# ELU steps whose relu VectorE takes from PSUM, and another order of all operations, in an attention kernel with a feed-forward layer behind it

## The chip, the cores and the metric

The kernel runs on one core of a Trainium2 chip. A core has five engines that each work through a queue of their own, in order: TensorE (PE in the profile, with PEld for its weight loads), VectorE (DVE), ScalarE (ACT), GpSimd (POOL) and SyncE (SP). They wait for each other by semaphores. Matrix products land in PSUM; ScalarE and VectorE carry them to SBUF. In this kernel POOL issues nearly all loads, SP issues the transposing loads and the stores. The metric is the time of one execution on the device, in microseconds.

## The reference

Eight batches of eight heads; 576 queries, 576 keys and 16 "beacon" keys that every query sees; the other keys are causal. The result of attention, 4608 tokens of 512 values, goes through a layer with an ELU between two products.

```python
def _attn_ref(q, k, v, beacon_k, beacon_v):
    B, H, S, D = q.shape                      # 8, 8, 576, 64
    k_all = np.concatenate([beacon_k, k], axis=2)
    v_all = np.concatenate([beacon_v, v], axis=2)
    scores = (1.0 / np.sqrt(D)) * np.matmul(q, k_all.transpose(0, 1, 3, 2))
    scores = np.where(causal, -1000000000.0, scores)
    a = np.exp(scores - scores.max(-1, keepdims=True))
    a /= a.sum(-1, keepdims=True) + 1e-09
    return np.matmul(a, v_all)

def _moe_ref(x, w_in, w_out):                 # 4608 x 512, 512 x 2048, 2048 x 512
    h = x @ w_in
    g = np.where(h > 0.0, h, np.exp(np.minimum(h, 0.0)) - 1.0)
    return g @ w_out
```

## The kernel before

The kernel is a set of small step functions and one long string of words, each word a step with its arguments. The program is issued in the order of that string, so every engine's queue is written out by hand: an engine does its share of the steps in the order in which they stand, and waits where a step's data or its buffer is not there yet. Neither a planner nor a loop decides at run time.

Attention, batch b: `lq` loads q and k (batches 0 to 2; `T` transposes them on TensorE, `cq` on VectorE or `ck` on ScalarE copies them out of PSUM), or `lk` copies them to a scratch in DRAM from which `lt` loads them transposed by DMA (batches 3 to 7); `cb` and `lp` put the beacon keys beside them. `lv` loads v in five pieces. `S` multiplies keys by queries, in the order of keys first, into a PSUM tile of two banks; `x` takes its exp on ScalarE; `m` masks on VectorE. The sums over the keys are matmuls with ones: `L` makes them for one group of four heads. For batches from BD = 3 on, `D` first adds the exps of the key blocks on VectorE, four additions for each pair of heads, so that `L` needs one matmul for each head in place of five. `n` makes the reciprocals (ln, then exp, on ScalarE), `W` multiplies v by the exps, and `M` scales the result into the tile `xT`. For batch 0 the work is cut into two halves, A and B.

The layer, tile t of 512 tokens (tiles 0 and 1 have 256): `F` makes one of 16 blocks of h in a PSUM bank of the tag hps, which has two. Then comes the ELU step of the block, in one of two forms. The usual one is `e` (exp, ScalarE, line 522), `u` (relu, ScalarE, line 527) and `k` (VectorE, line 537), min(exp - 1, relu). The one that spares ScalarE is `e`, then `r` on VectorE (min(exp, 1) - 1, line 545 for tiles 0 to 5 and line 549 for tiles 6 and 7), then `g` on VectorE (max of h from PSUM and r, line 554). The second product is `G` for tiles 0 and 1 (line 563) and `o`, `s` for the output. For tiles 2 to 9 it is a form of Strassen with seven products for eight: `Z` (VectorE) makes sums of blocks of g, `Q` (line 627) the matmuls, `J` takes partial results from PSUM, on ScalarE, or on VectorE where its word ends in `.v`. `wt` and `H` make the sums of weights. Tiles 8 and 9 use the same seven products for the first layer too: `X`, `P` (line 697), `K`, and the ELU of the blocks as `E`, `U` (ScalarE, line 726, or VectorE where the word ends in `.v`, line 728) and `V`.

`warm` and `wm` are dummy matmuls on zeros that keep TensorE busy in the head, four to a word. F.0.2 is the first step of the layer; all of the steps before it are called the head here. W.1.0 is batch 1's first product with v, L.2.0 batch 2's first step of sums that also reads v.

The buffers that matter: two PSUM tiles each for the tags S, hps and ops; three SBUF tiles for the exps and three for r and u. v has two buffers; so a third batch's load waits until the first batch's products are done.

Of the kernel before, what the change touches and what calls it, by code (L numbers as in the profile page):

```python
# [8 lines left out]
FP32 = mybir.dt.float32  # L9
# [8 lines left out]
def kernel(  # L18
# [11 lines left out]
    nc = tc.nc  # L30
# [144 lines left out]
    one32 = konst.tile([P, 1], FP32)  # L175
    nc.vector.memset(one32, 1.0)
# [225 lines left out]
    def L(b, g):  # L402
# [12 lines left out]
        else:  # L415
            t = hd[b, g] = psum.tile([P, 1024], FP32, tag="S", name="lt")
            r_ = lt[b, g] = t[:, 512 - QA:512 - QA + S]
            if b >= BD:
                for i in range(4):
                    nc.tensor.matmul(  # L420
                        out=r_[32 * i:32 * (i + 1), QA:S], lhsT=ones,
                        rhs=presum[b, 2 * g + i // 2][:, i % 2, QA:S], start=True, stop=True, skip_group_check=True)
            else:
                quad(b, g, QA, S, r_[:, QA:S], None, True)
# [91 lines left out]
    def flat(y):  # L516
        return y.rearrange("c n w -> c (n w)")
# [6 lines left out]
    @step  # L524
    def u(t, i):
        rb[t, i] = melt.tile([P, 512], FP16, tag="r", name="r")
        nc.scalar.activation(out=rb[t, i], in_=flat(hp[t, i]), func=AFT.Relu, bias=0.0, scale=1.0)  # L527
# [13 lines left out]
    @step  # L541
    def r(t, i):
        rb[t, i] = melt.tile([P, 512], FP16, tag="r", name="r")
        if t < 6:
            nc.vector.scalar_tensor_tensor(
                out=rb[t, i], in0=eb[t, i], scalar=1.0, in1=one32.to_broadcast([P, 512]),
                op0=ALU.min, op1=ALU.subtract)
# [243 lines left out]
    warm.4 warm.4 lq.0.0.0.4 lq.0.1.0.4 lv.0.2 warm.4 wm.4 ident T.0.0.0 bt ck.0.0.0 wm.4  # L791
    T.0.1.0 bk cb.0.2 cb.0.0 wm.4 lq.0.0.4.8 S.0.0.0 x.0.0.0 lq.0.1.4.8 T.0.0.1 lq.1.0.0.4 tri
    cq.0.1.0 cb.0.1 S.0.1.0 x.0.1.0 lv.0.0.1 T.0.1.1 wm.4 cq.0.0.1 S.0.0.2 x.0.0.2 S.0.0.1 wm.4
    cq.0.1.1 T.0.3.0 cb.0.3 x.0.0.1 cq.0.3.0 m.0.0.2 S.0.1.3 x.0.1.3 T.0.2.0 cq.0.2.0 S.0.1.1
    wm.4 x.0.1.1 T.0.2.1 S.0.3.0 wm.4 wm.4 x.0.3.0 T.0.3.1 cq.0.2.1 cq.0.3.1 S.0.2.0 wi.0
    S.0.2.3 x.0.2.0 wm.4 wm.4 x.0.2.3 wm.4 wm.4 m.0.0.0 m.0.2.0 m.0.1.0 S.0.3.1 x.0.3.1 wm.4
# [144 lines left out]
```

## Time and profile before

| | us |
|---|---|
| median of three runs | 334.65 (333.76, 334.65, 336.88) |
| the profiled execution, its own time | 336.74 |
| its span, first to last instruction | 335.0 |
| TensorE's mean granted clock | 0.993 of full speed |
| ScalarE, exps of the scores (line 336), 114 instructions | 105.7 |
| VectorE, k (line 537), 100 instructions | 67.0 |
| ScalarE, relu (line 527), 100 instructions | 61.9 |
| VectorE, g (line 554), 20 instructions | 13.7 |
| VectorE, r of tiles 0 to 5 (line 545), 14 instructions | 9.6 |

A row of a group gives the line, the engine, the operation, what it writes and reads, its shapes and its count, then the busy time, the mean of one in ns, and the time that the engine stood idle before such instructions with what ended it. A row of a stretch gives the busy time of each engine in it. The timeline gives start, length and what ran, in us from the start of the span. The profile is of one execution; the median is of others.

### The profile page before, as it was taken

The page shows a single profiled execution, that of the slowest core. Times are in us where ns is not written, and L with a number is a line of the kernel's source. Part 1 is how long each engine was busy: PE and PEld are TensorE (multiplying, and loading weights), DVE is VectorE, ACT ScalarE, POOL GpSimd, SP SyncE. Part 2 cuts the span into 40 slices and gives each one's busy share as a digit, 9 for nine tenths or more (in the row PEclk, how much of TensorE's full clock was granted, in tenths as well). Part 3 has the DMA queues.
Part 4 walks back from the last instruction along what each step waited for, and adds up shares of the span by engine and source line. Part 5 has one row for each costly group of instructions (what it writes and reads, how often), then busy time and mean ns, then how long its engine had stood idle before and what let it go on. Part 6 is the DMA issues. An engine that isn't in the chain of part 4 may idle for free.

```text
span 335.0 us, 8848 instructions
## 1 busy us (share of the span) xinstructions
PE 325.6 (97%) x3616; PEld 210.7 (63%) x3616; DVE 284.7 (85%) x601; ACT 278.1 (83%) x452; POOL 90.9 (27%) x117
## 2 busy tenths in 40 slices
PE   8899999999999999999999999999999999999994
PEld 3566766544455565656566656655666888788783
DVE  3555788875979999999899989998999999999982
ACT  2689999799999988999997998988987586889610
POOL 8968268630017284440061050000000000000000
PEclk9989999999999999999999999999999999999999
DMA  9999999999909999999199094320110110111112
GB/s 115 157 179 175 205 189 163 158 154 162 163 3 102 172 140 173 166 178 118 53 136 151 5 68 102 71 35 31 38 61 31 45 54 31 48 47 33 64 65 95
DMA packets 129113, 34.66 MB, mean 103 GB/s; under 512 B 112944, under 2 KB 127536, under 8 KB 129072
## 3 DMA queue, kind: packets, MB, share of 16 engines
q0 software_dynamic: 94944, 18.49, 68.8%
q1 hardware_dynamic: 33408, 15.34, 22.8%
q8 instruction: 28, 0.46, 0.6%
q10 hardware_dynamic: 720, 0.26, 0.3%
q14 instruction: 13, 0.11, 0.1%
HBM read 37.22 MB, written 15.34 MB: 157 GB/s over the span
## 4 chain that ended last, share of the span: by engine, by line
PE 87%; DVE 3%; ACT 3%; POOL 2%; DMA 2%; issue 1%; ACTq 0%; DVEq 0%; POOLq 0%
PE hps L512 30%; PE ops L627 29%; PE sc L321 8%; PE ut L378 6%; PE hps L697 5%; PE ops L563 4%; PE lt L378 2%; DMA kst<-in_k_dram 2%; ACT et L336 2%; POOL qst L136 1%; PE lt L420 1%; PE w L214 1%; PE tp L267 1%; PE ub L378 1%; DVE gt L554 1%
## 5 line engine op out<-in xcount | busy, mean ns | idle before, releaser
L512 PE MATMUL hps<-xT,w_in 128*128 128x512 f16 (+1 forms) x544 | 118.5, 354 | 0.3
L336 ACT ACTIVATE et<-sc 128x1024 f16<-128x1024 f32 (+2 forms) x114 | 105.7, 978 | 10.1 <-PE sc L321 9.5
L627 PEld LDWEIGHTS <-gt 128*128 128x128 f16 x768 | 73.3, 98 | 20.2 <-issue 3.7
L522 ACT ACTIVATE e<-hps 128x512 f32<-128x512 f32 x120 | 73.5, 620 | 13.8 <-PE hps L512 11.2
L512 PEld LDWEIGHTS <-w_in 128*128 128x128 f16 x544 | 50.6, 98 | 41.4 <-issue 4.4
L537 DVE SCALAR_TENSOR_TENSOR gt<-e,r 128x512 f16<-128x512 f32 x100 | 67.0, 684 | 8.0 <-ACT r L527 7.9
L527 ACT ACTIVATE r<-hps 128x512 f16<-128x512 f32 x100 | 61.9, 626 | 0.0
L627 PE MATMUL ops<-w_out,gt 128*128 128x256 f16 x384 | 50.7, 273 | 0.4 <-DVE gt L537 0.4
L627 PE MATMUL ops<-wt,gt 128*128 128x256 f16 x384 | 50.7, 273 | 0.0
L149 POOL DMA_DIRECT2D v<-in_v_dram x40 | 34.7, 919 | 5.0 <-DMA w_out<-in_moe_w_out_dram 2.7
L341 DVE TENSOR_TENSOR et<-et,triu 128x512 f16<-128x512 f16 (+4 forms) x108 | 31.2, 332 | 2.6 <-ACT et L336 2.4
L584 DVE TENSOR_TENSOR gt<-gt 128x1024 f16<-128x1024 f16 x48 | 32.4, 685 | 0.5
L378 PEld LDWEIGHTS <-v 128*32 128x32 f16 (+1 forms) x800 | 17.1, 96 | 10.6 <-issue 3.1
L394 DVE TENSOR_TENSOR qk<-qk,et 128x672 f16<-128x672 f16 (+2 forms) x60 | 21.2, 368 | 0.4
L378 PE MATMUL ut<-et,v 128*32 128x464 f16 (+3 forms) x560 | 20.9, 296 | 0.0
L472 DVE TENSOR_TENSOR xT<-ut,rl 128x672 f16<-128x672 f32 (+12 forms) x26 | 16.4, 670 | 3.1 <-PE ut L378 2.1
L643 DVE TENSOR_TENSOR osb<-ops,sm 128x512 f32<-128x512 f32 x24 | 16.4, 683 | 2.0 <-PE ops L627 1.9
L627 PE MATMUL ops<-w_out,s 128*128 128x256 f16 x128 | 17.1, 273 | 0.0
L563 PE MATMUL ops<-w_out,gt 128*128 128x512 f16 x64 | 16.0, 380 | 0.0
L736 DVE SCALAR_TENSOR_TENSOR gt<-e,r 128x512 f16<-128x512 f32 x24 | 15.9, 684 | 0.1
L627 PEld LDWEIGHTS <-s 128*128 128x128 f16 x128 | 12.3, 98 | 3.1 <-issue 0.3
L554 DVE TENSOR_TENSOR gt<-hps,r 128x512 f16<-128x512 f32 x20 | 13.7, 687 | 0.7
(111 smaller groups left out, 408.1 us busy)
## 6 DMA issues: line engine op xcount, KB each, us to landing
out_dram<-osb SPq DMA_DIRECT2D x35, 256.0 KB, 2.3
v<-in_v_dram POOLq DMA_DIRECT2D x24, 128.0 KB, 8.1
scr<-in_q_dram POOLq DMA_DIRECT2D x5, 576.0 KB, 15.6
scr<-in_k_dram POOLq DMA_DIRECT2D x5, 576.0 KB, 14.1
w_in<-in_moe_w_in_dram POOLq DMA_DIRECT2D x16, 128.0 KB, 5.9
w_out<-in_moe_w_out_dram POOLq DMA_DIRECT2D x4, 512.0 KB, 10.1
qst<-in_q_dram POOLq DMA_DIRECT2D x4, 288.0 KB, 8.7
kst<-in_k_dram POOLq DMA_DIRECT2D x4, 288.0 KB, 9.4
```

The costliest lines, as they stand in the source:

```text
L149: nc.gpsimd.dma_start(out=vt[b][r0:r0 + n, j, :, :], in_=v[b, :, ilo[j]:ilo[j] + n, :].rearrange("h s d -> s h d"),)
L321: nc.tensor.matmul(out=s[:, h, a - c0:e - c0], lhsT=t[D * h:D * (h + 1), 1, P * j:P * (j + 1)], rhs=t[D * h:D * (h + 1), 0, NB + qa + a - ...
L336: nc.scalar.activation(out=ets[b, d][:, :, a - EC2 * d:e - EC2 * d], in_=sc[b, g][:, :, a - c0:e - c0], func=AFT.Exp, bias=0.0, scale=SCALE)
L341: nc.vector.tensor_tensor(out=o, in0=o, in1=i, op=ALU.mult)
L378: nc.tensor.matmul(out=t[32 * i:32 * (i + 1), a - qa:e - qa], lhsT=ones[0:kc[j], :] if half is None else v16[0:kc[j], j, h, 32 * half:32 * ...
L512: nc.tensor.matmul(out=h[:, n_, :], lhsT=w_in16[:, cc, P * fc:P * (fc + 1)], rhs=xt[k][:, cc, a - TT * k:e - TT * k], start=(cc == 0), sto ...
L522: nc.scalar.activation(out=eb[t, i], in_=flat(hp[t, i]), func=AFT.Exp, bias=0.0, scale=1.0)
L527: nc.scalar.activation(out=rb[t, i], in_=flat(hp[t, i]), func=AFT.Relu, bias=0.0, scale=1.0)
L537: nc.vector.scalar_tensor_tensor(out=half(t, i), in0=eb[t, i], scalar=1.0, in1=rb[t, i], op0=ALU.subtract, op1=ALU.min)
L563: nc.tensor.matmul(out=ob[t, tb_], lhsT=gt[:, fc, P * tb_:P * (tb_ + 1)], rhs=w_out16[:, fc, :], start=(fc == 0), stop=(fc == NFC - 1))
L584: (nc.vector if eng == "v" else nc.gpsimd).tensor_tensor(out=o_, in0=a_, in1=b_, op=op_)
L627: nc.tensor.matmul(out=xy[t, n_][:, qd, :], lhsT=lw[:, P * qd:P * (qd + 1)], rhs=wt_[:, c, :], start=(first and qd == 0 and c == 0), stop= ...
```

## The change

Three things change. The ELU step that spares ScalarE in tiles 0 to 5 is no longer `e`, `r`, `g`: `u` gets an argument, and with `v` VectorE takes the relu from PSUM, always behind the exp of the same step; then comes `k`. In tiles 6 and 7 `r` and `g` stay, and the constant `one32` goes with the form that read it. Second, `L` takes the summed form for every pair of heads that has a `D`, not for batches from 3 on. Third, the string is another one.

```diff
-    one32 = konst.tile([P, 1], FP32)
-    nc.vector.memset(one32, 1.0)
@@ L
-            if b >= BD:
+            if (b, 2 * g) in presum:
@@ u
-    def u(t, i):
+    def u(t, i, eng="s"):
         rb[t, i] = melt.tile([P, 512], FP16, tag="r", name="r")
-        nc.scalar.activation(out=rb[t, i], in_=flat(hp[t, i]), func=AFT.Relu, bias=0.0, scale=1.0)
+        if eng == "s":
+            nc.scalar.activation(out=rb[t, i], in_=flat(hp[t, i]), func=AFT.Relu, bias=0.0, scale=1.0)
+        else:
+            nc.vector.tensor_scalar(out=rb[t, i], in0=flat(hp[t, i]), scalar1=0.0, scalar2=None, op0=ALU.max)
@@ r
-        if t < 6:
-            nc.vector.scalar_tensor_tensor(
-                out=rb[t, i], in0=eb[t, i], scalar=1.0, in1=one32.to_broadcast([P, 512]),
-                op0=ALU.min, op1=ALU.subtract)
-        else:
-            nc.vector.tensor_scalar(
-                out=rb[t, i], in0=eb[t, i], scalar1=1.0, scalar2=1.0, op0=ALU.min, op1=ALU.subtract)
+        nc.vector.tensor_scalar(
+            out=rb[t, i], in0=eb[t, i], scalar1=1.0, scalar2=1.0, op0=ALU.min, op1=ALU.subtract)
```

Counted by words, the string differs so:

| steps | before | after |
|---|---|---|
| `u` on ScalarE, tiles 0 to 7 | 92 | 80 |
| `u` on VectorE (`.v`) | 0 | 24, in tiles 0 (5), 1 (5), 2 (6), 3 (1), 4 (4), 5 (3) |
| `r` and `g`, tiles 0 to 5 | 14 | 0 |
| `r` and `g`, tiles 6 and 7 | 6 | 8 |
| `k` | 100 | 112 |
| `D` (batch 2's first group of heads has 8 of them after) | 80 | 88 |
| `wm` | 18 | 12 |
| first copy of the head | `ck.0.0.0` | `cq.0.0.0` |

Of `J`, eight words lose their `.v` and three get one; of `U`, six lose it and four get it. The other words are the same, in another order. The order of POOL's loads, up to the first of batch 4:

```
before: lq.0.0.0.4 lq.0.1.0.4 lv.0.2 ident lq.0.0.4.8 lq.0.1.4.8 lq.1.0.0.4 tri lv.0.0.1 wi.0 lv.0.3.4 wi.1
        lq.1.0.4.8 wo.0 lq.2.0.4.8 lq.2.0.0.4 wo.1 lv.1.0.1 wo.2 lv.1.2.3.4 lv.2.2.3.4 wo.3 lp.4.0 lk.3.0
        lv.2.0.1 lk.3.1 lp.3.0 lp.3.1 lk.4.1 lk.4.0
after:  lq.0.0.0.4 lq.0.1.0.4 ident lq.0.0.4.8 lq.0.1.4.8 tri lq.1.0.0.4 lv.0.2 lv.0.0.1 wi.0 lv.0.3.4 wi.1
        lq.1.0.4.8 wo.0 wo.2 lq.2.0.4.8 lq.2.0.0.4 wo.1 lv.1.0.1 lk.3.1 lv.1.2.3.4 wo.3 lk.3.0 lk.6.0
        lp.3.1 lp.4.0 lv.3.2.3.4 lv.2.2.3.4 lv.2.0.1 lv.3.0.1 lk.4.0
```

The steps around F.0.2 in the two strings:

```
before: L.0.A S.0.0.3 S.0.2.1 x.0.0.3 x.0.2.1 wm.4 S.0.3.2 x.0.3.2 T.1.0.0 n.0.A T.1.1.0 wm.4 wm.4 W.0.A.0
        cb.1.0 cq.1.0.0 m.0.2.3 S.1.1 m.0.1.3 m.0.1.2 m.0.3.2 cb.1.1 ck.1.1.0 x.1.1 wm.4 wm.4 S.1.2 W.0.A.1 x.1.2 S.0.3.3 x.0.3.3 S.0.2.2 m.0.0.3 x.0.2.2
        M.0.A.0 M.0.A.1 F.0.2 e.0.2 u.0.2 k.0.2 lv.0.3.4
after:  S.0.0.3 x.0.0.3 L.0.A T.1.0.0 n.0.A cq.1.0.0 cb.1.3 T.1.1.0 ck.1.1.0 wm.4 m.0.0.3 S.1.2 lv.0.2 lv.0.0.1
        W.0.A.1 M.0.A.1 x.1.2 S.1.1 x.1.1 W.0.A.0 M.0.A.0 S.0.3.3 x.0.3.3 S.0.2.2 wi.0 F.0.2 x.0.2.2 S.1.5
        S.1.0 m.0.1.2 e.0.2 m.0.2.2 u.0.2 k.0.2
```

More of the change, by code (lines that the diff above doesn't have):

```diff
@@ L790 @@
     run("""
[L791 to L796, printed above, removed]
@@ L911 @@
-    Q.9.84.91 J.9.4 Q.9.91.98 Q.9.98.105 J.9.5 Q.9.105.112 Jh.9.1 Jh.9.0
+    warm.4 lq.0.0.0.4 warm.4 lq.0.1.0.4 warm.4 wm.4 ident wm.4 T.0.0.0 bt wm.4 bk wm.4 wm.4
+    T.0.1.0 cb.0.0 cq.0.0.0 S.0.0.0 x.0.0.0 T.0.1.1 lq.0.0.4.8 cq.0.1.0 cb.0.1 S.0.1.0 x.0.1.0
+    cq.0.1.1 wm.4 wm.4 T.0.0.1 S.0.1.1 S.0.1.3 x.0.1.1 T.0.3.0 x.0.1.3 lq.0.1.4.8 cq.0.0.1
+    S.0.0.2 x.0.0.2 T.0.2.0 cq.0.3.0 S.0.0.1 x.0.0.1 cb.0.2 cq.0.2.0 cb.0.3 T.0.2.1 S.0.3.0
+    T.0.3.1 cq.0.2.1 S.0.2.0 x.0.3.0 S.0.2.3 tri x.0.2.0 x.0.2.3 m.0.1.3 cq.0.3.1 m.0.2.0
@@ new lines @@
+    F.5.3 k.5.12 e.5.3 u.5.3 S.6.10 S.6.0 x.6.0 x.6.10 Q.4.98.105 F.5.9 e.5.9 u.5.9 k.5.3
+    Q.4.105.112 k.5.0 m.6.0.0 Z.5.3.0 S.6.6 J.4.6.v D.6.0.0 x.6.6 Z.5.3.1 k.5.9 m.6.0.1 S.6.8
+    x.6.8 Q.5.0.7 F.6.11 e.6.11 r.6.11 F.6.4 e.6.4 u.6.4 Q.5.7.14 g.6.11 S.6.12 lt.7.1 x.6.12
+    m.6.1.1 S.7.2 x.7.2 Z.5.1.0 F.6.5 lp.7.0 F.6.6 D.6.1.1 D.6.1.2 Z.5.1.1 e.6.5 e.6.6 u.6.5
+    Q.5.14.21 Q.5.21.28 S.6.11 S.7.4 x.7.4 Z.5.2.0 r.6.6 g.6.6 k.6.4 Z.5.2.1 F.6.15 F.6.14
+    e.6.15 D.6.0.1 D.6.0.2 J.5.0 e.6.14 m.6.2.1 D.6.0.3 u.6.15 Z.5.4.0 x.6.11 S.6.7 x.6.7
```

225 lines of the change are left out of this document (111 added, 114 removed).

## Prediction

> **What bounds the kernel now.** I read the page's busy shares and chain first, then the sums by stretches of 15 us.
>
> ```profile
> PE 325.6 (97%) x3616; PEld 210.7 (63%) x3616; DVE 284.7 (85%) x601; ACT 278.1 (83%) x452; POOL 90.9 (27%) x117
> PEclk9989999999999999999999999999999999999999
> DMA  9999999999909999999199094320110110111112
> PE 87%; DVE 3%; ACT 3%; POOL 2%; DMA 2%; issue 1%; ACTq 0%; DVEq 0%; POOLq 0%
> 15.00:30.00 15.00, 13.90 (x274) 10.11 (x269) 8.03 (x28) 12.89 (x18) 10.90 (x20) 0.89 1.32 173
> 30.00:45.00 15.00, 14.73 (x265) 10.79 (x263) 10.86 (x20) 14.97 (x25) 7.94 (x11) 1.00 1.27 202
> 45.00:60.00 15.00, 14.85 (x232) 9.72 (x234) 12.76 (x29) 14.25 (x21) 11.53 (x17) 1.00 1.94 169
> 60.00:75.00 15.00, 14.96 (x184) 7.07 (x174) 11.85 (x27) 12.78 (x21) 7.17 (x5) 1.00 2.21 156
> 285.00:300.00 15.00, 15.00 (x125) 11.91 (x123) 14.69 (x26) 13.13 (x27) 0.00 (x0) 1.00 0.16 54
> 315.00:330.00 15.00, 14.62 (x124) 11.78 (x123) 11.48 (x19) 4.21 (x8) 0.00 (x0) 1.00 0.16 54
> 27.88 1.05 PE L512 MATMUL hps<-xT,w_in 128*128 128x256 f16 x8
> ```
>
> TensorE is busy for 97% of the 335.0 us and is 87% of the chain that ended last. The columns of the stretches are length, PE, PEld, DVE, ACT, POOL, clock, DMA share, GB/s. Between 30 and 75 us TensorE lacks 0.46 us (0.27 + 0.15 + 0.04), in the stretch at the end 0.38; the stretches between are full, as 285 to 300 shows. So behind F.0.2, the first matmul of the ELU part at 27.88, sparing another engine cannot buy more than about 1 us: matmuls would have to go. What can move is the head before 27.88, where ScalarE or a load ends most waits and dummy matmuls fill TensorE. From 30 to 45 us ScalarE has 0.03 us free, so a faster head holds only if ScalarE follows. The DMA engines stand at nine tenths for most of the first 160 us: a load moved ahead pushes the ones behind it.
>
> **The relus and the engines' sums.**
>
> ```profile
> L545 DVE SCALAR_TENSOR_TENSOR r<-e,one 128x512 f16<-128x512 f32 x14 | 9.6, 688 | 2.6 <-ACT e L522 2.4
> L554 DVE TENSOR_TENSOR gt<-hps,r 128x512 f16<-128x512 f32 x20 | 13.7, 687 | 0.7
> L537 DVE SCALAR_TENSOR_TENSOR gt<-e,r 128x512 f16<-128x512 f32 x100 | 67.0, 684 | 8.0 <-ACT r L527 7.9
> L527 ACT ACTIVATE r<-hps 128x512 f16<-128x512 f32 x100 | 61.9, 626 | 0.0
> L728 DVE TENSOR_SCALAR r<-hps x1: 692/692/692, 314.1 to 314.1; 128x512 f16<-128x512 f32 x1
> L636 ACT COPY sm<-ops x15: 576/587/740, 106.8 to 320.0; 128x512 f32<-128x512 f32 x15
> L636 DVE COPY sm<-ops x9: 676/683/692, 115.1 to 325.4; 128x512 f32<-128x512 f32 x9
> L394 DVE TENSOR_TENSOR qk<-et 128x928 f16<-128x928 f16 x20 | 12.5, 634 | 0.4 <-PE lt L420 0.3
> L394 DVE TENSOR_TENSOR qk<-qk,et 128x672 f16<-128x672 f16 (+2 forms) x60 | 21.2, 368 | 0.4
> ```
>
> Rows of groups: count | busy, mean ns | idle before. Of the 20 steps that spare ScalarE (r, then g), 14 lie in tiles 0 to 5, 6 in tiles 6 and 7; after, 24 u on VectorE lie in tiles 0 to 5 and 8 r/g behind them. No 24 such relus are in the trace; the one relu that VectorE takes from PSUM costs 0.69 (L728). VectorE loses 14 x 0.69 (r) and 12 x 0.69 (g), 17.9 us; it gains 24 x 0.69 (relus), 12 x 0.68 (k) and 2 x 0.69 at most (r of tiles 6 and 7), 26.1, and the sums D of batch 2: two pairs, each 0.63 + 21.2/60 x 3 = 1.69, 3.4 us. Five of the copies J leave it (-3.4), two net U (up to -1.4), one copy of the head comes (0.7). Sum +7.5: 284.7 becomes 292. ScalarE loses 12 x 0.62 of relus (-7.4), but takes five J at 0.60, two U at 0.62: -3.2, and one copy of the head (the price of a J, 0.6) less: 278.1 becomes about 274. So "sparing ScalarE" is mostly given back; that it does so little is seen in the order itself.
>
> Where does it lie? In tiles 0 to 2 VectorE gains 16 x 0.69 + 10 x 0.68 - 10 x 1.37 + 3.4 = 7.6 us, against 9.5 us (4.1 + 2.2 + 3.2) that it had free from 30 to 75: covered, and tight; without cover it would be paid on TensorE. ScalarE loses four relus of tiles 0 and 1, 2.5 us, just where it was full. Each relu waits for the exp of its step, and VectorE's queue (k, masks) stands behind it; r stood behind the same exp, 2.6 us idle in 14 (L545), so the wait is no new one. The PSUM bank is free when the relu ends, before g would have ended: nothing lost. From 75 us on TensorE has no idle time to win; J and U there cost 0.
>
> **The head** (gain). Rows of the timeline: start, length, engine, what, idle time before and its releaser.
>
> ```profile
> 15.49 0.86 ACT L336 ACTIVATE et<-sc 128x832 f16<-128x832 f32 x1 [1.84 <-PE sc L321]
> 16.91 1.62 ACT L336 ACTIVATE et<-sc 128x832 f16<-128x832 f32 x2 [0.55 <-PE sc L321]
> 19.55 3.89 ACT L336 ACTIVATE et<-sc 128x832 f16<-128x832 f32 x5 [1.02 <-PE sc L321]
> 4.20 0.57 POOL L144 DMA_DIRECT2D v<-in_beacon_v_dram x1
> 4.72 0.94 POOL L149 DMA_DIRECT2D v<-in_v_dram x1
> 14.82 0.33 PE L267 MATMUL tq<-identb,kst 80*64 80x80 bf16 x8 [0.93 <-DMA kst<-in_k_dram]
> L161 POOL DMA_DIRECT2D w_in<-in_moe_w_in_dram x8: 532/536/565, 13.4 to 19.8; - x8
> DMA to landing us min/median/max: 4.9/6.4/7.4
> ```
>
> ScalarE stands idle 3.4 us (1.84 + 0.55 + 1.02) between the exps of batch 0, first for the last k load of batch 0. lv.0.2 (0.57 + 0.94 us on POOL) now stands behind all loads of batch 0, and tri ahead of lq.1: those loads start 1.5 us earlier, so 14.82 becomes about 13.3. The later two gaps stood behind dummy matmuls and score steps that the new order places behind exps ready earlier. I leave 0.7 us of idle, and 0.3 for the first exp, whose copy (cq.0.0.0) now queues on VectorE behind bk and cb: 3.4 - 0.7 - 0.3 = 2.4 gained (all kept 3.1; only the load's share 1.2). F.0.2 comes at 25.5; w_in has landed by then (19.8 + 4.9 = 24.7). The 24 dummy matmuls dropped lie in waits: 0.
>
> **Batch 2's sums** (gain). L.2.0 drops 16 of its matmuls.
>
> ```profile
> 82.74 0.90 PE L378 MATMUL lt<-et,ones 128*32 128x464 f16 x24
> 83.46 0.27 PE L378 MATMUL lt<-et,v 128*32 128x112 f16 x8
> L420 PE MATMUL lt<-qk,ones 128*32 128x464 f16 x40 | 3.8, 365 | 0.0
> ```
>
> Its 24 matmuls take 0.72 (82.74 to 83.46); four on a sum take 0.38 (3.8 over ten groups), of which some overlaps: -0.4 us (0 to -0.5).
>
> **The loads** (loss). POOL's queue now has lk.3.1 ahead of lv.1.2.3.4, and lk.3.0, lk.6.0 and lv.3.2.3.4 ahead of batch 2's v.
>
> ```profile
> 61.56 2.83 PE L378 MATMUL ut<-et,v 128*32 128x464 f16 x80
> L149 POOL DMA_DIRECT2D v<-in_v_dram x3: 730/873/891, 42.5 to 45.1; - x3
> DMA to landing us min/median/max: 8.9/9.7/10.0
> L760 POOL DMA_DIRECT2D scr<-in_q_dram x1: 2201/2201/2201, 53.2 to 53.2; - x1
> DMA to landing us min/median/max: 9.3/9.3/9.3
> L760 POOL DMA_DIRECT2D scr<-in_k_dram x2: 2511/2614/2718, 56.6 to 59.6; - x2
> DMA to landing us min/median/max: 12.5/13.3/14.1
> L760 POOL DMA_DIRECT2D scr<-in_q_dram x1: 2190/2190/2190, 62.9 to 62.9; - x1
> DMA to landing us min/median/max: 14.1/17.4/20.7
> ```
>
> Before, v of batch 1 landed at 45.1 + 8.9 = 54.0, and W.1.0 read it at 61.56: 7.6 us of slack. One lk costs the queue 4.6 (69.1 = 56.6 + 12.5 to 73.7 = 59.6 + 14.1), so v lands at 58.6, less up to 0.8 for the earlier start of the queue: I take 58.2. W.1.0 comes earlier by 2.4 and by F.1.6 and L.1.1, now behind it (about 1.0 each): 57.2. A wait of 1.0 us (0 to 1.6), with all of TensorE queued behind. Batch 2's v: three v pieces take 1.5 for two steps (52.5 to 54.0), 0.75 each. lk.3.0 landed 8.5 behind v of batch 1 (62.5) with three v pieces between; now 6.2 behind, 64.4. Then lk.6.0 (4.6) and seven pieces (5.3): 9.9. L.2.0 needs the last at 83.46 - 2.4 - 1.1 (F.2.2 and S.2.9 now stand behind it) + 1.0 = 81.0. At full speed it lands at 74.3. The copies landing at 73.7 and, beside the transposes, at 83.6 (62.9 + 20.7), took 14.5 for two, 1.58 times as long: 80.0. No wait, 1.0 us to spare.
>
> The Trainium skill, "DMA: Bandwidth & Descriptors", Queues, rings and completion order, says that each DMA engine takes turns between the queues that have work, packet by packet; the copy that landed at 83.6 fits a halved share, the one at 73.7 does not. By the rule alone the outcome would be the slower rival below.
>
> **Sum.** -2.4 - 0.4 + 1.0 = -1.8. The profiled execution took 336.74 (335.0 of span, 1.7 around it): 334.9. The runs' median is 334.65, 2.1 below it: 332.8. This case runs from -3.1 - 0.5 (331.0) to 334.6 (only the load's 1.2 gained, and given back at W.1.0). No change that can be told is within 1%, 331.3 to 338.0; the three runs spread over 0.9%.
>
> **Rivals.**
> 1. Slower: the transposes (four, issued together once lk.3.0 has landed) halve POOL's queue for the whole stretch. 9.9 becomes 9.9 x 9.9/4.6 = 21.3, v of batch 2 lands at 85.7, L.2.0 waits 4.7; with lk.3.1 slowed in part, up to 7. Net +2.9 to +5.2: 337.6 to 339.9, taken as 338.8. It decides from 1.68 times (16.6 us). For: the copy of 9.9 us. Against: its neighbour of 4.6. Chance 0.17, as slower.
> 2. Nothing gained: TensorE's clock. The stretch 15 to 30 shows 0.89, that is 1.65 us of its work lost; PEclk dips in that slice alone. With 24 dummy matmuls fewer, a second such dip falls on the first ELU steps, or VectorE's 7.6 us don't fit: -1.8 + 1.65, 334.5. Against: the head has less waiting. Chance 0.15, within 1%. The Trainium skill, "TensorE: Matmul & The Clock Gate", What's actually happening, has idle time throttle the clock; the dip agrees, but no run here shows it with fewer dummies.
> 3. More gained: no wait at W.1.0, the head's whole 3.1, and the end's 0.38: -4.0, 330.6. For: loads on POOL may start 1.5 earlier throughout. Chance 0.20, faster.
>
> The forecast itself has 0.48, of which 0.06 below 331.3. Faster 0.26, within 1% 0.57, slower 0.17. The range leaves out half of rival 1 and of rival 3's lower side: 330.2 to 337.8.
>
> **What would show it.** Right: the first L512 at about 25.5, ScalarE's gaps between the exps under 1 us in all; a wait of v's load under 2 us at W.1.0; VectorE near 292 and ScalarE near 274; 3576 matmuls (24 dummies and 16 of L.2.0 fewer); the stretches past 75 us full. Wrong: L512 first at 27 or later; PE waiting for v or scr for over 2 us; PEclk below 9 in more slices; idle PE between 75 and 315.

## The result and the profile after

| | before | after |
|---|---|---|
| median of 20 executions, us | 334.99 (333.76 to 338.14) | 333.91 (332.92 to 334.96) |
| profiled execution, us (span) | 336.74 (335.0) | 333.87 (332.2) |
| mean clock granted in it | 0.993 | 0.999 |

The ratio is 0.9957, with a 95% interval of 0.9937 to 0.9978: 0.4% faster, within the 1% that was called no change. The two profiled executions lie 2.87 us apart, the medians 1.08. That gap between 2.87 and 1.08 is the first thing that the experiments had to explain.

Of the page of the changed kernel, the busy sums, clock, DMA share and the first line of the chain; then its sums by stretches (columns as in the prediction):

```profile
PE 322.4 (97%) x3576; PEld 208.4 (63%) x3576; DVE 291.6 (88%) x614; ACT 275.0 (83%) x446; POOL 88.7 (27%) x117
...
PEclk9999999999999999999999999999999999999999
DMA  9999999999989999953999099000100011011112
...
PE 80%; DMA 11%; POOL 3%; ACT 2%; issue 1%; DVE 1%; ACTq 0%; DVEq 0%; POOLq 0%
```

```profile
15.00:30.00 15.00, 12.81 (x278) 9.10 (x276) 9.19 (x36) 14.88 (x21) 10.42 (x18) 1.00 1.36 168
30.00:45.00 15.00, 14.64 (x248) 10.41 (x236) 13.33 (x22) 13.74 (x22) 8.39 (x12) 1.00 1.25 196
45.00:60.00 15.00, 14.89 (x270) 9.54 (x269) 12.43 (x30) 12.58 (x17) 10.59 (x15) 1.00 1.99 176
...
75.00:90.00 15.00, 14.96 (x167) 6.59 (x166) 14.37 (x31) 14.18 (x23) 3.86 (x4) 1.00 2.16 164
...
195.00:210.00 15.00, 14.83 (x118) 8.33 (x116) 14.44 (x30) 13.75 (x23) 2.80 (x4) 1.00 0.99 115
...
270.00:285.00 15.00, 14.84 (x157) 12.02 (x155) 14.26 (x26) 11.39 (x22) 0.00 (x0) 1.00 0.06 19
```

The reader should see three things. Work has gone from ScalarE to VectorE in the stretch from 30 to 45 us: ScalarE was full there (14.97 of 15) and now has 1.3 us free, VectorE rose from 10.86 to 13.33. (From 15 to 30 us ScalarE is now nearly full, 14.88.) The low digit in PEclk's row is gone. And DMA has 11% of the chain of waits, where it had 2%: loads now set part of the path.

The head, in the timeline (start, length, engine, what, idle time before):

```profile
9.93 1.62 ACT L334 ACTIVATE et<-sc 128x832 f16<-128x832 f32 x2 [7.84 <-PE sc L319]
11.90 9.18 ACT L334 ACTIVATE et<-sc 128x832 f16<-128x832 f32 x12 [0.36 <-PE sc L319]
...
25.42 1.05 PE L510 MATMUL hps<-xT,w_in 128*128 128x256 f16 x8
...
325.82 1.91 PE L623 MATMUL ops<-wt,gt 128*128 128x256 f16 x16
```

The first exp comes later than before (9.93 for 8.70), but the exps of batch 0 now run with one gap of 0.36 us in place of three that made 3.4, and F.0.2 starts at 25.42, 2.46 sooner than in the profiled execution of before. From there to the end of the last matmul (325.82 + 1.91 = 327.73) it takes 302.31 us. That length, from F.0.2 to the end of the last matmul, serves as a measure below; in the profile of before it is 302.70 (27.88 to 330.58). So by these two profiles 2.46 of the gain lie in the head and 0.39 behind it.

### The profile page after: what moved, and what is told of

It reads as the page before. It is cut to its first block, busy times and chain, and to the rows that moved or that the text cites. A ratio compares the mean times of both kernels' runs of the same rounds, so it can differ in the third digit from the quotient of the medians.

```text
span 332.2 us, 8763 instructions
## 1 busy us (share of the span) xinstructions
PE 322.4 (97%) x3576; PEld 208.4 (63%) x3576; DVE 291.6 (88%) x614; ACT 275.0 (83%) x446; POOL 88.7 (27%) x117
## 4 chain that ended last, share of the span: by engine, by line
PE 80%; DMA 11%; POOL 3%; ACT 2%; issue 1%; DVE 1%; ACTq 0%; DVEq 0%; POOLq 0%
PE ops L623 29%; PE hps L510 27%; PE sc L319 6%; PE ut L376 6%; PE hps L693 6%; PE ops L559 4%; DMA w_out<-in_moe_w_out_dram 3%; DMA w_in<-in_moe_w_in_dram 3%; DMA kst<-in_k_dram 2%; DMA v<-in_v_dram 2%; PE lt L376 1%; POOL qst L136 1%; ACT et L334 1%; PE lt L418 1%; POOL kst L136 1%
## 5 line engine op out<-in xcount | busy, mean ns | idle before, releaser
L334 ACT ACTIVATE et<-sc 128x1024 f16<-128x1024 f32 (+2 forms) x114 | 103.6, 978 | 11.8 <-PE sc L319 11.8
L538 DVE SCALAR_TENSOR_TENSOR gt<-e,r 128x512 f16<-128x512 f32 x112 | 75.5, 685 | 5.8 <-ACT r L526 5.0
L526 ACT ACTIVATE r<-hps 128x512 f16<-128x512 f32 x88 | 54.3, 619 | 0.0
L623 PE MATMUL ops<-w_out,gt 128*128 128x256 f16 x384 | 49.9, 273 | 0.0
L392 DVE TENSOR_TENSOR qk<-qk,et 128x672 f16<-128x672 f16 (+2 forms) x66 | 23.3, 368 | 0.5
L144 POOL DMA_DIRECT2D v<-in_beacon_v_dram x8 | 4.8, 594 | 62.7 <-PE lt L376 48.6
L528 DVE TENSOR_SCALAR r<-hps 128x512 f16<-128x512 f32 x24 | 16.5, 686 | 3.2 <-ACT e L520 3.2
L632 ACT COPY sm<-ops 128x512 f32<-128x512 f32 x20 | 12.1, 607 | 4.8 <-PE ops L623 4.8
```

Source lines behind the costliest of these rows:

```text
L334: nc.scalar.activation(out=ets[b, d][:, :, a - EC2 * d:e - EC2 * d], in_=sc[b, g][:, :, a - c0:e - c0], func=AFT.Exp, bias=0.0, scale=SCALE)
L392: (nc.vector if eng == "v" else nc.gpsimd).tensor_tensor(out=o, in0=t[0:rows, :, a:e] if n == 0 else o, in1=t[0:rows, :, col:col + e - a], ...
L538: nc.vector.scalar_tensor_tensor(out=half(t, i), in0=eb[t, i], scalar=1.0, in1=rb[t, i], op0=ALU.subtract, op1=ALU.min)
L623: nc.tensor.matmul(out=xy[t, n_][:, qd, :], lhsT=lw[:, P * qd:P * (qd + 1)], rhs=wt_[:, c, :], start=(first and qd == 0 and c == 0), stop= ...
```

## The experiments

Each kernel was timed beside the kernel before on the same chip, in 12 executions (6 for the relus on ScalarE). "Behind F.0.2" is the measure just described, in the profiled execution of that run.

| kernel | median, us | ratio to before (95%) | F.0.2 at | behind F.0.2 |
|---|---|---|---|---|
| before, again | 335.04 | 1.0004 (0.9972 to 1.0035) | 25.99 | 302.70 |
| after, again | 333.56 | 0.9934 (0.9906 to 0.9962) | 24.28 | 303.13 |
| after, third time | 334.22 | 0.9955 (0.9923 to 0.9987) | 25.10 | 302.89 |
| before with the new head | 334.15 | 0.9953 (0.9921 to 0.9985) | 24.53 | 302.70 |
| before with lv.0.2 moved | 333.80 | 0.9961 (0.9938 to 0.9983) | 24.88 | 302.69 |
| before with relus from PSUM | 335.01 | 1.0017 (0.9983 to 1.0050) | 26.15 | 302.36 |
| after with lv.0.2 back | 334.52 | 0.9977 (0.9947 to 1.0007) | 25.08 | 303.40 |
| after with r and g as before | 337.45 | 1.0048 (1.0025 to 1.0072) | 24.56 | 306.87 |
| after with those relus on ScalarE | 340.97 | 1.0162 (1.0126 to 1.0198) | 25.47 | 309.76 |
| after without sums of batch 2 | 334.29 | 0.9964 (0.9933 to 0.9994) | 25.32 | 302.65 |
| after with loads undone | 333.48 | 0.9952 (0.9925 to 0.9978) | 24.60 | 302.02 |
| after, loads undone, first exp sooner | 333.93 | 0.9948 (0.9921 to 0.9975) | 24.59 | 303.44 |

**Both kernels again, unchanged.**

> The kernel before, unchanged. In its profiled execution PEclk dips in one slice of the head (0.50 of the clock for about 3.4 us from 16 us on), and that execution took 336.74 us, 1.75 above the median. Theory 1: such a window falls into some of its executions and costs each of them 1.7 to 2.5 us; the others have the first matmul of F.0.2 (L512) near 26.3, not 27.9, so the head that the change really shortens is worth about 1 us. Then the times form two groups, the one near 334.4 with a mean clock of 0.998 or more, the other 336 to 338 with 0.994 or less. Theory 2: the head costs 27.9 us in every execution, and the change loses 1.4 us of its 2.5 later, in executions other than the profiled one. Then time doesn't follow the clock, and an execution at clock 0.999 still has L512 at 27.5 or later.

> The changed kernel, unchanged. Theory 1: 333.9 us, no execution above 335.5, L512/L510 of F.0.2 at 25.4 within 0.4, TensorE's busy time behind it as in the first profile. Theory 2: executions spread because v of batch 1 lands right at its use (57.2): the profile shows a wait for v of 0.5 us or more in front of W.1.0 and a longer time behind F.0.2 (302.3 us in the first profile).

Theory 1 holds for the kernel before. The experiments brought three sets of its executions. 97 of them are counted here (the two longest, 339.29 and 339.68 us, both at clock 0.988, are left out); ordered by their mean clock they fall into two groups with no overlap in time:

| chip | clock 0.996 or more: executions, median us | clock 0.995 or less: executions, median us |
|---|---|---|
| first | 18, 334.84 | 17, 336.83 |
| second | 25, 334.60 | 9, 336.94 |
| third | 18, 334.53 | 10, 337.07 |

All 61 of the first group lie at 335.36 or below, all 36 of the second at 336.17 or above. Within the second group time follows the clock too: the 26 executions at 0.991 to 0.995 have a median of 336.77, the ten at 0.987 to 0.989 one of 337.95. The changed kernel's 44 executions, over all its runs, reach 335.69 at most; four stand at 0.994 or 0.995, and the slowest of those took 334.59. A mean just under 1 need not mean a loss: in 12 of the 14 profiles the clock also falls to half behind the last matmul, 2.0 to 3.7 us after it, where no work is left to slow, and in the second profile of the changed kernel this alone makes the mean 0.996. What the window is can be read in the first profile of before, by microseconds (length, PE, PEld, DVE, ACT, POOL, clock, DMA share, GB/s):

```profile
16.00:17.00 1.00, 1.00 (x28) 0.82 (x28) 0.57 (x2) 0.45 (x2) 0.53 (x1) 0.64 2.04 169
17.00:18.00 1.00, 1.00 (x13) 0.84 (x10) 0.94 (x6) 1.00 (x2) 0.45 (x1) 0.50 2.08 176
18.00:19.00 1.00, 1.00 (x12) 0.80 (x12) 1.00 (x8) 0.53 (x1) 0.62 (x2) 0.50 1.31 207
19.00:20.00 1.00, 1.00 (x13) 0.55 (x12) 0.56 (x5) 0.45 (x1) 0.19 (x1) 0.65 1.09 199
```

PE looks full in every line, but between 17 and 20 it issues 12 or 13 matmuls per microsecond: at half clock, TensorE looks busy and gets less done. The timeline has 16 dummy matmuls in 1.89 us there, from 17.16 on, and 8 in 0.62 ahead of it, from 15.38 on. The losses 0.36, 0.50, 0.50 and 0.35 make 1.71 us, that is one window of 3.4 us at half clock. The second profile of before has none, and shows what the head is without it:

```profile
8.57 0.86 ACT L336 ACTIVATE et<-sc 128x832 f16<-128x832 f32 x1 [1.13 <-PE sc L321]
9.89 0.86 ACT L336 ACTIVATE et<-sc 128x832 f16<-128x832 f32 x1 [0.46 <-PE sc L321]
10.95 3.13 ACT L336 ACTIVATE et<-sc 128x832 f16<-128x832 f32 x4 [0.19 <-PE sc L321]
14.90 0.86 ACT L336 ACTIVATE et<-sc 128x832 f16<-128x832 f32 x1 [0.82 <-PE sc L321]
16.15 5.40 ACT L336 ACTIVATE et<-sc 128x832 f16<-128x832 f32 x7 [0.39 <-PE sc L321]
...
14.23 0.33 PE L267 MATMUL tq<-identb,kst 80*64 80x80 bf16 x8 [0.53 <-DMA kst<-in_k_dram]
...
25.99 1.05 PE L512 MATMUL hps<-xT,w_in 128*128 128x256 f16 x8
```

ScalarE's gaps behind the first exp are 0.46 + 0.19 + 0.82 + 0.39 = 1.86 us here, not 3.4. F.0.2 comes 1.89 sooner than in the first profile (25.99 for 27.88). Of this 0.59 is there before the window begins: the transposes of the last k load stand at 14.23 for 14.82, the exp behind them at 14.90 for 15.49. The other 1.30 arises from the window on. Behind F.0.2 the two profiles of before agree to the hundredth, 302.70.

The changed kernel is another matter. Its F.0.2 moved by 1.14 us between its first two profiles, its last matmul by 0.32 (327.73 and 327.41). The second profile shows where the early start is lost:

```profile
24.28 1.05 PE L510 MATMUL hps<-xT,w_in 128*128 128x256 f16 x8
...
35.47 0.45 PE L265 MATMUL tp<-identb,kst 96*64 96x96 bf16 x12 [0.42 <-DMA kst<-in_k_dram]
...
79.03 0.28 PE L376 MATMUL lt<-et,v 128*32 128x112 f16 x8 [0.47 <-DMA v<-in_v_dram]
...
325.50 1.91 PE L623 MATMUL ops<-wt,gt 128*128 128x256 f16 x16
```

T.1.2.0 waits 0.42 us for k of batch 1 (lq.1.0.4.8), L.2.0 0.47 for v of batch 2. In front of W.1.0, where theory 2 put a wait of 0.5 or more, the timeline shows none. The wait is inside W.1.0: its weight loads stop for the last piece of v of batch 1, and its matmuls take 0.26 us longer than in the first profile (1.77 for 1.51):

```profile
57.22 0.69 PEld L376 LDWEIGHTS <-v 80*32 80x32 f16 x24 [0.38 <-DMA v<-in_v_dram]
```

So theory 2 is right for the changed kernel in kind, with smaller waits and more places: 303.13 for 302.31 us behind F.0.2.

**Only the head.** The order up to F.0.2 from the changed kernel, the rest from before:

```diff
-    warm.4 warm.4 lq.0.0.0.4 lq.0.1.0.4 lv.0.2 warm.4 wm.4 ident T.0.0.0 bt ck.0.0.0 wm.4
+    warm.4 lq.0.0.0.4 warm.4 lq.0.1.0.4 warm.4 wm.4 ident wm.4 T.0.0.0 bt wm.4 bk wm.4 wm.4
...
-    x.0.2.2 M.0.A.0 M.0.A.1 F.0.2 e.0.2 u.0.2 k.0.2 lv.0.3.4
+    M.0.A.0 S.0.3.3 x.0.3.3 S.0.2.2 wi.0 F.0.2 x.0.2.2 m.0.1.2 e.0.2 u.0.2 k.0.2 m.0.0.2 lv.0.3.4
```

> The kernel before with the changed kernel's order up to F.0.2 and its own order from there on. Theory 1 (all of the gain but 0.4 us lies in the head): 334.2 us, 0.4 above the changed kernel, L512 of F.0.2 at 25.4, no execution above 335.5, and the time from F.0.2 to the end 302.7 us as before. Theory 2 (the head brings 2.5 and the rest of the changed order takes 1.4 back): 332.5 us.

F.0.2 came at 24.53, the rest took 302.70, and the ratio (0.9953) can't be told from the changed kernel's 0.9934 on that chip. As far as the times can tell, the head holds the gain. Theory 1 holds but for two executions in 12: one stood at clock 0.994 and took 338.12, one took 335.58 at 0.998. The new head makes the slow executions rarer, not impossible.

**One word moved, in the kernel before** (lv.0.2, which issues beacon v and the first piece of v of batch 0).

```diff
-    warm.4 warm.4 lq.0.0.0.4 lq.0.1.0.4 lv.0.2 warm.4 wm.4 ident T.0.0.0
+    warm.4 warm.4 lq.0.0.0.4 lq.0.1.0.4 warm.4 wm.4 ident T.0.0.0
...
-    T.0.0.1 lq.1.0.0.4 tri
+    T.0.0.1 lq.1.0.0.4 tri lv.0.2
```

> The kernel before with one word moved: lv.0.2 (the first v load of batch 0) stands behind the q and k loads of batch 0 and behind tri. Theory 1 (the waits of TensorE for the last q and k loads of batch 0 are what lets the clock down to 0.50 a few us later): the DMA waits of 0.5 to 0.9 us at 13 to 15 us are gone, no execution has a mean clock under 0.996, L512 of F.0.2 comes at 25.2 (25.99 in the second profile of before), median 334.1. Theory 2 (dummy matmuls and the order of the score steps decide): the waits are gone, but about half of the executions still stand at clock 0.995 or below and above 336, median 335.

```profile
8.95 5.71 ACT L336 ACTIVATE et<-sc 128x832 f16<-128x832 f32 x7 [1.13 <-PE sc L321]
15.04 5.40 ACT L336 ACTIVATE et<-sc 128x832 f16<-128x832 f32 x7 [0.39 <-PE sc L321]
...
24.88 1.05 PE L512 MATMUL hps<-xT,w_in 128*128 128x256 f16 x8
```

This single word does nearly all that the change does for the time: ratio 0.9961, none of 12 executions below clock 0.997, the waits for the last q and k loads gone, F.0.2 1.1 us sooner at 24.88 and 302.69 behind it. All 18 dummy words stand where they stood, so the dummies didn't decide it. Ahead of the window of the first profile of before, TensorE had waited for the last k load (0.93 us, shown with the prediction) and for the last q load:

```profile
13.56 0.33 PE L267 MATMUL tq<-identb,qst 80*64 80x80 bf16 x8 [0.60 <-DMA qst<-in_q_dram]
```

How long it was kept from work there is in the sums of 10 to 15 us, of the first profile of before and then of the second, which had no window:

```profile
10.00:15.00 5.00, 3.35 (x60) 1.97 (x58) 2.27 (x5) 3.53 (x5) 4.92 (x9) 1.00 1.28 156
```

```profile
10.00:15.00 5.00, 4.38 (x88) 2.80 (x81) 3.17 (x7) 3.99 (x6) 4.92 (x10) 1.00 1.28 163
```

TensorE was busy for 3.35 us of 5 in the one, for 4.38 in the other. The Trainium skill, "TensorE: Matmul & The Clock Gate", What's actually happening, has the clock halved after at least one idle window of about 3.4 us, on windows that run by themselves and don't start with the kernel. The length agrees (1.71 us lost at half clock), and that only some executions are hit would fit free-running windows. But no idle of 3.4 us stands ahead of it here: the longest wait in these 5 us was 0.93 us, the two together 1.53. So in this kernel a window with waits in it, not an idle one, was enough. The end of the second profile of the changed kernel agrees: half clock begins there only 2.0 us after the last matmul. That these waits decide it is shown only so far that moving this load took both away together: the second profile of before had one of 0.53 us and no window.

**The same load back, in the changed kernel.**

```diff
-    warm.4 lq.0.0.0.4 warm.4 lq.0.1.0.4 warm.4 wm.4 ident wm.4 T.0.0.0
+    warm.4 lq.0.0.0.4 warm.4 lq.0.1.0.4 lv.0.2 warm.4 wm.4 ident wm.4 T.0.0.0
...
-    m.0.0.3 S.1.2 lv.0.2 lv.0.0.1 W.0.A.1
+    m.0.0.3 S.1.2 lv.0.0.1 W.0.A.1
```

> The changed kernel with lv.0.2 back in its old place, ahead of the identity and of the later loads of batch 0, all else as it is (24 dummy matmuls fewer than before, the new order of the score steps). Theory 1 (the waits for the last q and k loads let the clock down): waits of 0.5 us or more for qst or kst at 13 to 15 us are back, and in about half of the executions the mean clock is 0.995 or less and the time 2 us higher; median 335. Theory 2 (the load's place costs only its own 1.2 us of ScalarE, and the clock goes with the dummies): F.0.2 about 1 us later, no execution at 0.993 or less, median 334.4.

Neither theory held whole. The waits for q and k are not back: the transposes of that last load ran at 13.43 and 13.66 without one, just behind its landing at 12.8 and 13.6. F.0.2 came at 25.08, no later than in the changed kernel. The median rose by 0.30 over the changed kernel on that chip (334.52 and 334.22; ratios 0.9977 and 0.9955, intervals that overlap). Two of 12 executions stood at 0.976 and 0.981, lower than any of before (0.987 at the least), and took only 336.60 and 335.83; a third stood at 0.993 and took 334.78. Why is open. In the new order no worth of this load's place is shown.

**The form of the relu, in the order of before.**

```diff
-    r.1.1 S.1.3 cb.1.2 x.1.3 g.1.1
+    u.1.1.v S.1.3 cb.1.2 x.1.3 k.1.1
```

and so for all 14 such steps of tiles 0 to 5.

> The kernel before, order unchanged, but its 14 steps of tiles 0 to 5 that ran r and g on VectorE take the relu from PSUM on VectorE in r's place and k in g's place. Theory 1 (there the old form cost no wait, since the order was made for it): the time from F.0.2 to the end stays at 302.7, VectorE's sum at 284.5, the median that of before. Rival (24 steps of the old form cost the changed kernel 3.9 us, 0.16 each, so 14 cost 2): 333 us, 2 below before.

Nothing: 1.0017, with 1 inside the interval, VectorE at 284.7, 302.36 behind F.0.2. In that order the form is free.

**The old form, in the order of after.**

```diff
-    F.0.3 e.0.3 S.1.4 u.0.3.v k.0.3 x.1.4
+    F.0.3 e.0.3 S.1.4 r.0.3 g.0.3 x.1.4
```

and so for all 24, with r as it was for tiles below 6.

> The changed kernel, with each of the 24 steps whose relu VectorE reads from PSUM turned back to the old form: r (0.69 us, from SBUF) and g (0.69 us, from PSUM), both at the relu's place; the k of these steps goes. Theory 1 (the form of the relu is worth nothing, TensorE being full): within 0.5 us of the changed kernel, VectorE's sum within 1 us of 291.6. Rival (the relu from PSUM matters, because the bank comes free 0.69 us earlier than with r and g): 1 us or more slower, with PE waits for g in the trace between 28 and 75 us.

The rival is right, and by more than it said: 3.9 us over the changed kernel on the same chip. VectorE's sum is 292.4, 0.7 more, so it isn't VectorE's work. Its groups for g and r, the longest of TensorE's waits (engine, line, what it waited for: us in total, times, longest), and three of these in the timeline:

```profile
L557 DVE TENSOR_TENSOR gt<-hps,r 128x512 f16<-128x512 f32 x32 | 22.1, 691 | 1.6
L548 DVE SCALAR_TENSOR_TENSOR r<-e,one 128x512 f16<-128x512 f32 x24 | 16.5, 687 | 2.5 <-ACT e L522 2.4
```

```profile
PE hps L512 <- DVE gt L557: 2.8, 7, 0.8
```

```profile
35.20 1.03 PE L512 MATMUL hps<-xT,w_in 128*128 128x256 f16 x8 [0.58 <-DVE gt L557]
...
42.65 1.03 PE L512 MATMUL hps<-xT,w_in 128*128 128x256 f16 x8 [0.62 <-DVE gt L557]
...
77.50 1.02 PE L512 MATMUL hps<-xT,w_in 128*128 128x512 f16 x4 [0.78 <-DVE gt L557]
```

A bank of hps is read last by g here, 0.69 + 0.69 = 1.38 us of VectorE after the exp, and by the relu after 0.69 in the changed kernel. There are two such banks, and the F step that wants one back waits for g: 2.8 us in seven waits, most of the 3.9. What the form buys is the bank, 0.69 us sooner each time; what makes the rest of the 3.9 was not taken apart.

**Those relus on ScalarE.**

```diff
-    F.0.3 e.0.3 S.1.4 u.0.3.v k.0.3 x.1.4
+    F.0.3 e.0.3 S.1.4 u.0.3 k.0.3 x.1.4
```

and so for all 24.

> The changed kernel with its 24 relus from PSUM on ScalarE (0.62 us each) in place of VectorE (0.69), at the same places; k stays. ScalarE's sum rises by 14.9 us to 290, VectorE's falls by 16.5 to 275. Theory 1 (where the order puts them, ScalarE is full between 10 and 50 us, so sparing it is what lets TensorE run): TensorE waits for exps and relus, 2 to 4 us slower than the changed kernel, most of it for the 13 relus ahead of 65 us. Rival (TensorE is the bound and either engine has room): within 0.5 us.

6.75 us slower than the changed kernel on that chip (340.97 and 334.22), beyond theory 1's 2 to 4. Its two largest waits, and the worst stretch:

```profile
PE sc L319 <- ACT et L334: 3.9, 7, 1.5
PE hps L510 <- ACT r L526: 3.3, 5, 1.0
```

```profile
45.00:60.00 15.00, 12.43 (x206) 8.10 (x205) 10.22 (x24) 13.27 (x20) 10.59 (x9) 1.00 1.96 176
```

TensorE loses 2.57 us of these 15 alone. The sums of the engines tell little of this: ScalarE is busy for 84% of the span, and even in this stretch it has 1.73 us free. Single exps and relus come too late. The sums came out at 285.7 (ScalarE) and 277.2 (VectorE), where 290 and 275 had been expected. And not most of the loss lies ahead of 65 us, but about half: against the changed kernel TensorE loses 2.9 us more from 30 to 75 us and 3.0 more from 75 to 315.

**Batch 2's sums.** The changed kernel with its eight words D.2 dropped:

```diff
-    F.2.6 S.2.4 k.0.7 e.2.6 S.2.5 D.2.0.0 F.2.11
+    F.2.6 S.2.4 k.0.7 e.2.6 S.2.5 F.2.11
```

> The changed kernel without the sums D of batch 2 on VectorE: L.2.0 multiplies all its columns again, as before. Theory 1: L.2.0 takes 0.43 us longer, so the median rises by 0.4 over the changed kernel, to 334.0; VectorE's sum falls by 3.4 to 288.3. Rival: L.2.0 waits for v of batch 2 anyway, so the sums hid nothing or little there: within 0.1 of the changed kernel.

What the sums save in L.2.0 can be read from its first matmul with ones to its first with v, here and then in the third profile of the changed kernel:

```profile
78.89 0.90 PE L376 MATMUL lt<-et,ones 128*32 128x464 f16 x24
79.62 0.27 PE L376 MATMUL lt<-et,v 128*32 128x112 f16 x8
...
79.38 0.38 PE L418 MATMUL lt<-qk,ones 128*32 128x464 f16 x4
79.63 0.27 PE L376 MATMUL lt<-et,v 128*32 128x112 f16 x8
```

That is 0.73 us without the sums and 0.25 with them, 0.48 saved. In the other two profiles of the changed kernel it is 0.47 and 0.89, because L.2.0 then waits for v of batch 2. So theory 1 has the matmuls right, and the rival is right that a late v can take the gain back. Neither the medians (ratio 0.9964 and, for the changed kernel's three runs, 0.9934 to 0.9957) nor the time behind F.0.2 (302.65, between the changed kernel's 302.31 and 303.13) can confirm 0.4 us. VectorE's sum fell by 2.5, to 289.1, where 288.3 had been expected.

**The loads of batches 1 to 3.**

```diff
-    F.0.7 lk.3.1 S.2.1
+    F.0.7 S.2.1
...
-    wo.3 k.0.5
+    wo.3 lk.3.1 k.0.5
...
-    F.2.14 lk.6.0 e.2.11 ... S.2.6 lv.3.2.3.4 H.1.0 ... lt.3.0 lv.2.2.3.4 D.2.1.3 F.2.15 lv.2.0.1 lt.3.1
+    F.2.14 e.2.11 ... S.2.6 lv.2.2.3.4 lv.2.0.1 H.1.0 ... lt.3.0 lv.3.2.3.4 D.2.1.3 F.2.15 lk.6.0 lt.3.1
```

> The changed kernel with the loads of batches 1 to 3 in an order like before's: lk.3.1 behind lv.1.2.3.4 and wo.3; v of batch 2 ahead of v of batch 3; lk.6.0 behind both. In the second profile of the changed kernel, F.0.2 came at 24.3, 1.1 sooner than in the first, but the end only 0.3 sooner: TensorE waited 0.47 us for v of batch 2 in L.2.0, some 0.3 more than usual in W.1.0. Theory 1 (these loads give back part of the head): both waits go, the time from F.0.2 to the end is 302.3 or less when F.0.2 comes at 24.3, and the median is 332.9, 0.7 below the changed kernel. Rival (POOL's queue is full anyway, and the wait only moves to another load): no more than 0.2 us, with a wait for lk.3's or w_out's load in place of v's.

In the trace theory 1 holds: no wait for a load of v is left, and with F.0.2 at 24.60 the rest takes 302.02, the shortest of all. The wait of T.1.2.0 is gone too, though the edit does not touch its load, so not all of the difference is the edit's. In the times nothing is shown: 0.9952 against the changed kernel's 0.9934 to 0.9957.

**The loads undone, and the first exp sooner.**

```diff
-    ident wm.4 T.0.0.0 bt wm.4 bk wm.4 wm.4 T.0.1.0 cb.0.0 cq.0.0.0 S.0.0.0
+    ident T.0.0.0 bt ck.0.0.0 wm.4 T.0.1.0 bk cb.0.0 wm.4 S.0.0.0
```

> The changed kernel again, as the measure for the next three on the same chip: 333.6 us within 0.4, clock 0.995 or more and no execution above 335.5. F.0.2 at 24.3 to 25.4, behind it 302.3 us where it comes late and up to 303.1 where it comes early.

> The changed kernel with the loads of batches 1 to 3 as in the run before with such loads, and a shorter way to the first exp: ck.0.0.0 on ScalarE, idle there, in place of cq.0.0.0 on VectorE behind bk and cb.0.0, and eight dummy matmuls fewer ahead of T.0.1.0. Theory 1 (the head is ScalarE's chain of exps): first exp 0.7 us sooner, F.0.2 as much, 332.2 us, 1.4 below the changed kernel (0.7 of it from the loads). Rival (the head is bound by loads: the first half of w_in lands at 24.2 to 25.2, and F.0.2 at 24.56 has waited 0.5 for it in one run): the first exp comes sooner, F.0.2 doesn't, 332.9.

The changed kernel's third median, 334.22, lies 0.2 beyond what was expected, and two of its executions took 335.67 and 335.69 at clock 0.998 or more. On this chip its times spread over 3.1 us (332.60 to 335.69) at a mean clock of 0.994 or more; the cause of that is not known. In its third profile the waits for loads are there again, the longest in T.1.2.0, one inside W.1.0:

```profile
36.56 0.45 PE L265 MATMUL tp<-identb,kst 96*64 96x96 bf16 x12 [0.69 <-DMA kst<-in_k_dram]
...
58.46 0.88 PE L376 MATMUL ut<-et,v 80*32 80x80 f16 x24 [0.23 <-DMA v<-in_v_dram]
```

The kernel with both edits took 333.93, ratio 0.9948 against 0.9955 on the same chip: no difference that can be told. Its timeline:

```profile
9.09 1.62 ACT L334 ACTIVATE et<-sc 128x832 f16<-128x832 f32 x2 [1.13 <-PE sc L319]
...
24.59 1.11 PE L510 MATMUL hps<-xT,w_in 128*128 128x256 f16 x8
...
31.53 1.24 PE L376 MATMUL ub<-et,v 128*32 128x320 f16 x37 [1.03 <-issue]
```

The first exp came 0.52 us sooner than in the changed kernel beside it (9.09 and 9.61), F.0.2 as much (24.59 and 25.10), as theory 1 has it; the end did not follow, for a stall of 1.03 us in W.0.B that the profile gives to no engine and no DMA. So its forecast of 332.2 failed, and the rival's load in front of F.0.2 isn't what held it. No version here beats the changed kernel by more than the intervals.

## Why the prediction was right, and where it was not

No change beyond 1% was the likeliest outcome and is what came; 333.91 lies in the forecast case's own range, 1.1 us above the 332.8 given. Step by step:

**The head, -2.4.** This is the step that failed: at full clock the head gives 1.1. The profiled difference is 2.46, but that it agrees is luck: the three gaps of ScalarE that the step adds up (3.4 us) were read in an execution with a half-clock window in their midst. The two later gaps (0.55 + 1.02), put down to dummy matmuls and the order of the score steps, lie in that window, where the other profile has 0.39; the first (1.84) has a k load that came 0.59 later than in the other. In an execution without the window the gaps are 1.86 in all. F.0.2 then moves from 25.99 and 26.15 (before, and before with the new relus) to 24.28, 25.10 and 25.42, 1.1 us by the means. The first exp came at 8.79, 9.61 and 9.93, where 9.0 had been put.

**The load's share of it, 1.2.** Right: lv.0.2 moved alone brought F.0.2 from 25.99 to 24.88. That the rest of the new head adds to this is not shown.

**The sum, taken off the median.** A gain read in an execution with the window can't be taken off a median of executions that mostly lack it. At clock 0.996 or more the kernel before has a median of 334.64 (61 executions); the changed kernel's 44 have 333.92: 0.7 us gained (1.3 on the first chip, 0.3 on the third). The other part of the gain is the executions at a lower clock: 36 of 97 of before took 2.3 us more (336.96 as their median, less 334.64), some 0.9 in the mean, and the changed kernel hardly has them. That the window in the head is the cause in all 36 is taken from one profile. The profiles give 1.1 from the head and nothing net behind it: 302.78 as the mean of the changed kernel's three, 302.70 before; the waits for late loads are of the size of what batch 2's sums save.

**The relus.** Their price (0.69; 0.686 measured) and the sums (292 and 274; 291.6 and 275.0) were right, and so was "no new wait". But "mostly given back" read the sums and not the places: without its sparing of ScalarE the new order is 6.75 us slower, and with the old form of it 3.9. That the bank comes free sooner was noted as no loss; in the new order, with 24 such steps, it is most of the 3.9.

**Batch 2's sums, -0.4.** The matmuls of L.2.0 are 0.48 shorter where v is there in time, 0.26 in the first profile, and in the second L.2.0 is longer than before (0.89 for 0.73); the times neither confirm nor deny it.

**The loads, +1.0 at W.1.0.** v of batch 1 was put at 58.2 and needed at 57.2. In the first profile of after, the issues of its last pieces, the step that reads them, and the one weight load of TensorE that waits for a v:

```profile
L149 POOL DMA_DIRECT2D v<-in_v_dram x2: 735/1072/1408, 45.8 to 47.2; - x2
...
DMA to landing us min/median/max: 10.0/10.4/10.9
```

```profile
57.15 1.51 PE L376 MATMUL ut<-et,v 128*32 128x464 f16 x40
```

```profile
79.35 0.12 PEld L376 LDWEIGHTS <-v 128*32 128x32 f16 x8 [0.35 <-DMA v<-in_v_dram]
```

It landed at 57.2 (47.2 + 10.0), as W.1.0 began, a microsecond sooner than put, and W.1.0 did not wait for it; in the second and third profiles its last piece cost 0.26 and 0.23 us, where up to 1.6 had been allowed. The 0.35 is at L.2.0, for v of batch 2, where 1.0 us to spare was reckoned; the second profile has 0.47 there, the third none. T.1.2.0 waited 0.42 and 0.69 for k in the second and third, which was not foreseen. An earlier head meets loads that keep their own time.

**The rivals.** The slower one came to 0.47 us at L.2.0, not 4.7 to 7. The second had the clock the wrong way round: in the changed kernel fewer dummies went with fewer dips, and one load moved, with every dummy in place, went with none in 12 executions; and VectorE's 7.6 us did fit. The third needed the head's whole 3.1, which was not there.

**The signs.** The first L512 at 25.42 for 25.5, one gap of 0.36 between the exps, a wait for v under 2 us and 3576 matmuls were all as written; the stretches past 75 us lack 0.04, 0.17 and 0.16 us in three places where before lacked nothing, and no longer the 0.38 at the end. So one of the signs of being wrong, idle TensorE between 75 and 315, is there, but small. The sign for the head was fulfilled by two profiles that differed in their clock: a sign that agrees doesn't show the cause.

## What to carry to other kernels

Before a gap is priced, look at the granted clock in the same microseconds, and at whether other executions of the same kernel have that window: a median and a profiled execution may not be of one kind. An engine that is a few per cent from full is worth sparing by the place and not by the sum, and of two forms that cost the same, the one that lets go of a PSUM bank sooner can be the better (3.9 us in the new order here, nothing in the old). A head made shorter is worth only as much as the loads behind it are early.

## What the runs showed of the hardware that was not expected

- A window of half clock of some 3.4 us fell into the head of one profiled execution of before and not of the other; 36 of 97 executions of this program stood at a mean clock of 0.995 or less and took 2.3 us longer by the medians. When one word with two loads was moved and every dummy matmul left in place, none of 12 executions stood below 0.997.
- Half clock began 2.0 to 3.7 us after the last matmul in 12 of the 14 profiles; the mean clock counts this stretch, the work doesn't feel it.
- In two kernels W.0.B stalled for 0.89 and 1.03 us with no releaser ("issue" in the timeline, at about 31 us), and in the three profiles of the changed kernel it did not. Its cause is open.
